# Joining turned token planes on ScalarE, and turning the fourth expert's tokens by DMA, in a mixture of experts behind banded attention

## The chip, the cores and the metric

The kernel runs on one core of one Trainium2 chip. The metric is the device time of one execution in microseconds (us); of several runs the median stands for the kernel. The engines are TensorE (PE in the profile; its weight loads are PEld), VectorE (DVE), ScalarE (ACT), GpSimd (POOL) and SyncE (SP), which issues most of the DMA transfers. GpSimd issues the indirect ones: it gathers rows by a list of indices and scatters them.

## The reference

The input is q, k and v of 8 batches, 8 heads, 576 positions and 64 columns. Attention looks back over a band of 128 positions, with a bias that falls linearly with the distance. Its output, 4608 tokens of 512 columns, goes through eight experts with room for 576 tokens each:

```
scores = where(mask, scale * q @ k.T + bias, -1e9);  x = softmax(scores) @ v
logits = x @ w_gate
for idx in argsort(-logits.flatten()):          # all pairs of token and expert, best first
    tok, e = idx // 8, idx % 8
    if assigned[tok] >= 0 or counts[e] >= 576: continue
    assigned[tok] = e; counts[e] += 1
for e in range(8):
    out[assigned == e] = maximum(x[assigned == e] @ w1[e], 0) @ w2[e]     # 512 -> 1024 -> 512
```

The assignment is greedy over all pairs, so which tokens an expert gets depends on which experts are full already.

## The kernel before, in words

The first part of the span is attention, which writes x to DRAM and the logits to SBUF. Then the router works in eight phases. Each phase finds which expert fills next and the list of its tokens; phase k + 1 runs while expert k is computed. The experts are worked in the order in which they fill. Below they are e0 to e7 in that order, so e3 is the fourth.

**One expert** has two layers, L1 and L2. A matmul of two float32 values is made of three matmuls of their rounded high and low parts. L1 (function `layer1`, matmuls on L1059) works on 8 blocks f of 128 hidden columns, each of two halves of 288 tokens and 12 matmuls a half: 192 matmuls of 288 columns. ScalarE writes the high part of the block (hh, L1064) with the relu, VectorE the low part (hlo, L1069). The halves go through four banks of PSUM. L2 (`layer2`, L1087, L1088, L1090) works on 5 blocks t of 128 tokens (the last has 64), 112 matmuls of 512 columns; ScalarE copies each block from the bank po into o (L1094), VectorE does so for the last, and GpSimd scatters it to the output (L1099). Weights are loaded by SP, eight chunks for an expert, and split into high and low parts by ScalarE (L965) and VectorE (L967, two halves).

**The tokens** of the next expert are gathered by GpSimd, five tiles of 128 (the last of 64), as rows of 512 columns (g, L976). L1 needs them with columns across partitions: they have to be turned. For e1, e2 and e3 TensorE turns them (`turn`, L1000): four 128x128 transposes a tile into the bank pg, from which ScalarE takes the high part xh (L1003) and VectorE the low part xl (L1004). For e4 to e7 (`turn_by_dma`) GpSimd splits each float32 tile into two planes of 16-bit halves (pl, L1017, two copies a tile), SP turns both by one DMA transfer (tp, L1022), GpSimd joins the halves to float32 words again (xf, L1029, two copies a tile), and ScalarE and VectorE take xh (L1037) and xl (L1038). g, pl, tp and xf share one ring of seven buffers.

**The router's steps** are a chain between VectorE and TensorE: VectorE builds compare results and one-hot rows (among them L586, ind; L812, loOH; L808 and L809, mv), TensorE counts with them (L610, L630, L786, L787), and the last step (L817, 18 short matmuls of 128x40) makes the list of tokens out of loOH and mv.

**The order.** Expert k's matmuls are cut into slots, i = 0 to 15 in L1 (12 matmuls) and 16 to 30 in L2 (nine matmuls, six where t is 4). At the end of each slot the function `slot(k, i)` puts other work into the program by tables: `W_LOAD` and `W_SPLIT` say at which slot of which expert a chunk of weights is loaded and split, `WAITS` how many slots lie between two steps of the router, and `DMA_AT` at which slots the generator `turn_by_dma` is taken a step further: its first step issues the gathers, the next five split, the next five turn, and the rest join and take high and low parts. `BY_DMA` is the first expert k in whose time the next one's tokens are turned by DMA. A scheduler then sets the order of every engine's own queue out of this program and its model of times; each engine works its queue strictly in that order. A dependency of the kind `BEHIND` only tells this scheduler to put one instruction behind another. Such a one puts the turning transfers behind the last weight load of L2.

Of the kernel before, what the change touches and what calls it, by code (L numbers as in the profile page):

```python
# [6 lines left out]
F32R = mybir.dt.float32r  # L7
# [3 lines left out]
AF = mybir.ActivationFunctionType  # L11
# [6 lines left out]
CAP = N // E  # L18
# [403 lines left out]
WAITS = (2, 1, 3, 1, 1, 3, 3)  # L422
TURN_WAIT, TURN_STEP = (6, 3), (1, 2)
TURN0 = 3
BY_DMA = 3
DMA_AT = [0, 1, 1, 2, 2, 2, 7, 7, 7, 7, 7, 9, 9, 10, 10, 10, 17, 19, 21, 23, 25]
BEHIND = mybir.DependencyInfo(mybir.DependencyClass.NoSync, mybir.DependencyReason.SCHED_ONLY)
BIG = 1e30
MAGIC = 12582912.0
# [11 lines left out]
def bc(ap, shape):  # L441
    return ap.to_broadcast(shape)
# [17 lines left out]
class Router:  # L460
# [255 lines left out]
    def phase(self, k, exact=False):  # L716
        nc, rt, rs = self.nc, self.p["rt"], self.p["rs"]
# [93 lines left out]
        for a, z in ((0, 18), (18, 30), (30, NT)) if k == 0 else ((0, NT),):  # L811
            nc.vector.tensor_tensor(loOH[:, a:z], bc(self.C["i64"].rearrange("p (s o) -> p s o", o=2).unsqueeze(1), [128, z - a, 32, 2]),  # L812
                                    bc(slo[:, a:z].unsqueeze(2), [128, z - a, 32, 2]), ALU.is_equal)
        yield WAITS[6] + (k < 4)
        ip = self.bank()
        for c in range(0, NT, 2):
            self.last_pe = nc.tensor.matmul(ip[:, 0:40], loOH[:, c:c + 2].rearrange("p c s o -> p (c s o)"),  # L817
# [11 lines left out]
        if k < 7:  # L829
            self.pen = self.small("pen", 8)  # L830
            nc.vector.tensor_scalar(self.pen, Dc, float(CAP), -BIG, ALU.is_ge, ALU.mult)
            self.base = self.small("base", 8)
            nc.vector.tensor_tensor(self.base, self.pen, Dc, ALU.add)
            nc.vector.scalar_tensor_tensor(self.left, keyv, mx[:, 0:1], self.left, ALU.not_equal, ALU.mult)
            L2 = rt.tile([128, 8, NT], F32, name="L2", bufs=1)
            eng = nc.vector if k == 0 or k > BY_DMA else self.tc.nc.gpsimd
            eng.tensor_tensor(L2, L, bc(self.pen.unsqueeze(2), [128, 8, NT]), ALU.add)
            if k == 0 or k > BY_DMA:
                nc.vector.scalar_tensor_tensor(self.L1, T1, 100.0 * BIG, L2, ALU.mult, ALU.add)
            else:  # L840
                Lt = rt.tile([128, 8, NT], F32, name="Lt", bufs=1)
                eng.tensor_scalar(Lt, T1, 100.0 * BIG, 1.0, ALU.mult, ALU.mult)
                eng.tensor_tensor(self.L1, Lt, L2, ALU.add)
# [103 lines left out]
class MoE:  # L947
# [60 lines left out]
    def turn_by_dma(self, idx, asked):  # L1008

        nc, ring = self.nc, self.p["g"]  # L1010
        gs, pls, tps, xfs = self.gather(idx), [], [], []
        yield
        for g, r in gs:
            pl = ring.tile([128, 2, DM], U16, name="pl", tag="g")
            words = g.bitcast(U16).rearrange("q (c o) -> q c o", o=2)
            for a in range(2):
                nc.gpsimd.tensor_copy(pl[:r, a, :], words[:r, :, 1 - a])  # L1017
            pls.append((pl, r))
            yield
        for pl, r in pls:  # L1020
            tp = ring.tile([128, 8, 128], U16, name="tp", tag="g")
            asked.append(nc.sync.dma_start_transpose(tp[:, :, :r], pl[:r].rearrange("q a c -> q (a c)")))  # L1022
            tps.append((tp, r))
            yield
        for tp, r in tps:
            xf = ring.tile([128, 4, 128], F32, name="xf", tag="g")
            words = xf.rearrange("q j t -> q (j t)").bitcast(U16).rearrange("q (j t o) -> q j t o", j=4, o=2)
            for a in range(2):
                nc.gpsimd.tensor_copy(words[:, :, :r, 1 - a], tp[:, 4 * a:4 * a + 4, :r])  # L1029
            xfs.append((xf, r))  # L1030
            yield
        xh = self.p["xg"].tile([128, 4, CAP], F32R, name="xh")
        xl = self.p["xg"].tile([128, 4, CAP], F32R, name="xl")
        self.xg = xh, xl
        for h, (xf, r) in enumerate(xfs):
            o = slice(128 * h, 128 * h + r)
            nc.scalar.copy(xh[:, :, o], xf[:, :, :r])  # L1037
            nc.vector.tensor_tensor(xl[:, :, o], xf[:, :, :r], xh[:, :, o].bitcast(F32), ALU.subtract)  # L1038
            yield

    def layer1(self, w1, xg, first=False):
        nc = self.nc
        xh, xl = xg

        hh = self.p["h"].tile([128, 8, 640], F32R, name="hh")
        hl = self.p["h"].tile([128, 8, 512], F32R, name="hlo")
        cut = (0, 256, 576) if first else (0, 288, 576)
        order = [(f, (0, 1)) for f in range(8)] if not first else [(f, (t,)) for t in range(2) for f in range(8)]
        for f, ts in order:
            w = w1[f // 2].rearrange("p a (j f) -> p a j f", j=4)  # L1050
            fo = (f % 2) * 128
            pp = {t: self.p["ps_h"].tile([128, 512], F32, name="ph")[:, 0:cut[t + 1] - cut[t]] for t in ts}
            todo = [(j, a, x) for j in range(4) for a, x in ((0, xh), (0, xl), (1, xh))]
            if first and f == 0:

                todo.sort(key=lambda p: p[2] is xl)
            for i, (j, a, x) in enumerate(todo):
                for t in ts:
                    nc.tensor.matmul(pp[t], w[:, a, j, fo:fo + 128], x[:, j, cut[t]:cut[t + 1]], start=(i == 0), stop=(i == 11))  # L1059
                if i == 5 and len(ts) == 2:  # L1060
                    yield
            for t in ts:
                o = hh[:, f, cut[t]:cut[t + 1]]
                nc.scalar.activation(o, pp[t], AF.Relu)  # L1064
                e = min(512, cut[t + 1])
                for c0, c1, d in ((cut[t], e, hl[:, f, cut[t]:e]), (e, cut[t + 1], hh[:, f, 576:640])):
                    if c0 < c1:
                        c0, c1 = c0 - cut[t], c1 - cut[t]
                        nc.vector.scalar_tensor_tensor(d, pp[t][:, c0:c1], 0.0, o[:, c0:c1].bitcast(F32), ALU.max, ALU.subtract)  # L1069
            yield  # L1070
        self.h = hh, hl

    def layer2(self, w2, h, idx, last=False):
        nc = self.nc
        hh, hl = h
        for t in range(5) if not last else (4, 0, 1, 2, 3):
            r = 128 if t < 4 else 64

            cols = (slice(0, 256), slice(256, 512)) if last and t == 3 else (slice(0, 512),)
            o = self.p["o"].tile([128, DM], F32, name="o")  # L1080
            for cs in cols:
                po = self.p["ps_o"].tile([128, 512], F32, name="po")
                for f in range(8):
                    w = w2[f // 2].rearrange("p a (c d) -> p a c d", c=2)
                    wh, wl = w[:, 0, f % 2, cs], w[:, 1, f % 2, cs]
                    a, out = hh[:, f, 128 * t:128 * t + 128], po[:, cs]
                    nc.tensor.matmul(out, a, wh, start=(f == 0), stop=False)  # L1087
                    nc.tensor.matmul(out, a, wl, start=False, stop=(f == 7 and t == 4))  # L1088
                    if t < 4:
                        nc.tensor.matmul(out, hl[:, f, 128 * t:128 * t + 128], wh, start=False, stop=(f == 7))  # L1090
                    if f in (2, 5):
                        yield
                if t < 4:
                    nc.scalar.copy(o[:, cs], po[:, cs])  # L1094
                else:
                    o2 = self.p["o"].tile([64, DM], F32, name="o2", bufs=1)
                    nc.vector.tensor_copy(o2, po[64:128, :])
                    nc.vector.tensor_tensor(o[0:64, :], po[0:64, :], o2, ALU.add)
            self.sent = nc.gpsimd.indirect_dma_start(out=self.out, out_offset=bass.IndirectOffsetOnAxis(ap=idx[:r, t:t + 1], axis=0),  # L1099
                                              in_=o[:r, :], in_offset=None)  # L1100
            yield
# [49 lines left out]
def layer_moe(tc, P, C, r, x, w1, w2, out, exact):  # L1151
# [26 lines left out]
    st = dict(wait=START, turn=0)  # L1178
    raws, loaders = {}, {}

    def slot(k, i):
# [18 lines left out]
        for e, layer, c, due in W_SPLIT:  # L1200
            e += k
            if i >= due and len(W.get((e, layer), (0,) * 9)) == c and len(raws[e, layer]) > c:
                W[e, layer].append(m.split(raws[e, layer][c]))
                break
        if k >= BY_DMA and k + 1 in r.idx:
            if k not in gathers:
                asked[k + 1] = []
                gathers[k], st["made"] = m.turn_by_dma(r.idx[k + 1], asked[k + 1]), 0
            while st["made"] < len(DMA_AT) and i >= DMA_AT[st["made"]]:
                next(gathers[k])  # L1210
                st["made"] += 1
        elif i >= 16 and k + 1 in r.idx:
            if k not in gathers:
                gathers[k], st["turn"] = m.turn(m.gather(r.idx[k + 1])), i + TURN_WAIT[min(k, 1)]
            elif i >= st["turn"]:
                next(gathers[k], None)
                st["turn"] = i + TURN_STEP[min(k, 1)]

    gathers, asked = {}, {}
    for k in range(E):  # L1220
        i = 0
# [96 lines left out]
```

## Time and profile before

| | before |
|---|---|
| median of 3 runs | 692.46 us (691.09 to 694.73) |
| the profiled execution | 690.85 us |
| its span, first to last instruction | 688.9 us |
| TensorE busy, mean granted clock | 657.4 us (95%), 0.984 |
| VectorE, ScalarE, GpSimd busy | 479.1 (70%), 332.1 (48%), 192.7 us (28%) |
| L1 and L2 of e2 begin | 356.64 and 385.30 us |
| L1 and L2 of e3 | 415.99 and 443.80 us |
| L1 and L2 of e4 | 471.17 and 498.25 us |
| L1 and L2 of e5 | 526.54 and 553.11 us |
| L1 and L2 of e6, L1 and L2 of e7 | 579.48, 605.06, 630.47 and 656.05 us |

Times in the rows of the profile are us from the start of the span. A row of the timeline gives start, duration, engine, line, operation, what is written and read, shapes and count (neighbours of one kind are put together), and in brackets how long the engine stood before it and what released it. A row of the groups gives line, engine, operation, shapes and count, then busy us and mean ns, then the engine's idle time before such instructions and its releasers. Matmuls are pipelined: one starts before the one ahead of it has ended.

### The profile page before, as it was taken

To read this page: it belongs to the slowest core of one execution; us is meant where nothing else is said; L and a number is where in the kernel's file an instruction comes from. 1 tells how busy PE (TensorE), PEld (TensorE's weight loads), DVE (VectorE), ACT (ScalarE), POOL (GpSimd) and SP (SyncE) were. 2 spreads that over 40 slices of the span, in tenths; PEclk is the share of its full clock that TensorE was granted. 3 is DMA by queue.
4 is the path that set the end of the run, shared out by engine and by line. 5 is a ranking of instruction groups with operands and counts; after the bars stand their busy time and mean duration, and the time that the engine had idled before them with its cause. 6 is when DMAs were issued, how large, how long until landed. Compare 5 with 4: busy or idle time off the path is not lost.

```text
span 688.9 us, 18916 instructions
## 1 busy us (share of the span) xinstructions
PE 657.4 (95%) x7171; PEld 582.2 (85%) x7172; DVE 479.1 (70%) x1985; ACT 332.1 (48%) x991; POOL 192.7 (28%) x376
## 2 busy tenths in 40 slices
PE   7999999999995699999999999999989999999995
PEld 4898998998985399889789779979978978988985
DVE  5788888888887899879669788886775734532310
ACT  6898888888884262334134224324323333432210
POOL 4021221211220301511422017255076075152011
PEclk9999999999997799999999999999999999999998
DMA  8456566566532453615417227635625644621001
GB/s 307 148 181 202 175 193 200 166 211 186 161 106 70 124 191 104 241 39 187 158 36 245 88 92 245 131 106 182 133 98 166 167 111 169 160 52 54 1 25 49
DMA packets 54212, 97.47 MB, mean 141 GB/s; under 512 B 22880, under 2 KB 32224, under 8 KB 54112
## 3 DMA queue, kind: packets, MB, share of 16 engines
q1 hardware_dynamic: 48224, 77.30, 37.0%
q0 software_dynamic: 5888, 18.88, 8.3%
q8 instruction: 58, 0.95, 0.6%
q14 instruction: 42, 0.34, 0.1%
HBM read 72.57 MB, written 18.87 MB: 133 GB/s over the span
## 4 chain that ended last, share of the span: by engine, by line
PE 77%; DVE 12%; DMA 6%; issue 2%; ACT 1%; SPq 1%; POOL 0%; POOLq 0%; DVEq 0%; ACTq 0%
PE ph L1059 20%; PE po L1087 9%; PE po L1088 9%; PE s L54 8%; PE pt L54 7%; PE pt L158 7%; PE po L1090 7%; PE x L54 6%; DMA raw<-in_w_dram 2%; DVE hl L967 2%; DMA tp<-pl 1%; DVE hlo L1069 1%; DMA craw<-in_cst_dram 1%; PE pg L1000 1%; DMA qk<-in_qk_dram 1%
## 5 line engine op out<-in xcount | busy, mean ns | idle before, releaser
L1059 PE MATMUL ph<-xh,hl 128*128 128x288 f32 (+2 forms) x1024 | 188.9, 299 | 0.7 <-DVE lo L534 0.5
L1059 PEld LDWEIGHTS ph<-xh,hl 128*128 128x128 f32 x1024 | 154.7, 189 | 2.4 <-ACT hh L1064 1.0
L145 ACT ACTIVATE u<-u,mn 128x192 f32<-128x192 f32 (+2 forms) x288 | 123.9, 433 | 24.6 <-DVE mn L134 24.5
L1087 PE MATMUL po<-hl,hh 128*128 128x512 f32 (+1 forms) x328 | 128.9, 393 | 0.6 <-ACT o L1094 0.6
L1088 PE MATMUL po<-hl,hh 128*128 128x512 f32 (+1 forms) x328 | 126.4, 385 | 0.0
L967 DVE TENSOR_TENSOR hl<-raw,hl 128x512 fp32r<-128x512 f32 x128 | 88.1, 708 | 48.6 <-ACT hl L965 48.1
L1059 PE MATMUL ph<-xl,hl 128*128 128x288 f32 (+2 forms) x512 | 115.1, 297 | 0.0
L1064 ACT ACTIVATE hh<-ph 128x288 fp32r<-128x288 f32 (+2 forms) x128 | 46.6, 408 | 131.9 <-PE ph L1059 128.8
L134 DVE CUSTOM_DVE_ANT_0 u<-s,bm 128x192 f32<-128x192 f32 x308 | 86.5, 333 | 29.8 <-PE s L54 29.2
L1090 PE MATMUL po<-hl,hlo 128*128 128x512 f32 (+1 forms) x264 | 101.3, 384 | 0.0
L1099 POOL DMA_INDIRECT out_dram<-o,idx x40 | 42.5, 1063 | 153.1 <-ACT o L1094 76.0
L1059 PEld LDWEIGHTS ph<-xl,hl 128*128 128x128 f32 x512 | 84.1, 189 | 0.0
L965 ACT CAST hl<-raw 128x1024 fp32r<-128x1024 f32 x64 | 65.8, 1050 | 25.1 <-DMA raw<-in_w_dram 22.0
L1069 DVE SCALAR_TENSOR_TENSOR hlo<-ph,hh 128x288 fp32r<-128x288 f32 (+2 forms) x128 | 49.4, 417 | 35.8 <-ACT hh L1064 35.1
L1087 PEld LDWEIGHTS po<-hl,hh 128*128 128x128 f32 x328 | 61.8, 188 | 12.3 <-ACT o L1094 1.0
L54 PE MATMUL s<-qk 64*64 64x192 f32 (+1 forms) x1112 | 69.6, 319 | 2.5 <-DVE mn L134 1.8
L1088 PEld LDWEIGHTS po<-hl,hh 128*128 128x128 f32 x328 | 61.8, 188 | 11.0
L1094 ACT COPY o<-po 128x512 f32<-128x512 f32 (+1 forms) x33 | 18.8, 572 | 95.7 <-PE po L1090 77.4
L976 POOL DMA_INDIRECT g<-x,idx x40 | 42.1, 1053 | 72.2 <-issue 31.7
L1090 PEld LDWEIGHTS po<-hl,hlo 128*128 128x128 f32 x264 | 49.6, 188 | 10.0
L158 PE MATMUL pt<-ident_sb,u 128*128 128x128 f32 x368 | 54.2, 282 | 1.4 <-DVE mn L134 1.0
L54 PEld LDWEIGHTS s<-qk 64*64 64x64 f32 x1112 | 48.3, 132 | 8.3 <-issue 2.2
(240 smaller groups left out, 925.8 us busy)
## 6 DMA issues: line engine op xcount, KB each, us to landing
raw<-in_w_dram SPq DMA_DIRECT2D x64, 512.0 KB, 4.4
qk<-in_qk_dram SPq DMA_DIRECT2D x32, 576.0 KB, 4.8
v<-in_v_dram SPq DMA_DIRECT2D x32, 288.0 KB, 3.8
x<-xb SPq DMA_DIRECT2D x14, 512.0 KB, 3.5
x<-xb SPq DMA_DIRECT2D x8, 128.0 KB, 3.3
x<-xb SPq DMA_DIRECT2D x4, 256.0 KB, 2.4
g<-x,idx POOLq DMA_INDIRECT x40, 3.9
out_dram<-o,idx POOLq DMA_INDIRECT x40, 3.2
```

The costliest lines, as they stand in the source:

```text
L54: put(nc.tensor.matmul(out, w, a, start=start, stop=stop, skip_group_check=True))
L134: put(nc.vector.tensor_tensor_reduce(out=u[rows], in0=x[rows, c:c + 64 * m].rearrange("q (j k) -> q j k", k=64), in1=bm[n % NP][rows, y:y ...
L145: put(nc.scalar.activation(u, u, AF.Exp, bias=st["mn"][:, i:i + 1], scale=-1.0, accum_out=st["sm"][:, i:i + 1]))
L158: put(nc.tensor.transpose(ps[:, c:c + 128], u[:, o + 128 * j:o + 128 * j + 128], ident))
L965: self.last = nc.scalar.copy(hl[:, 0, :], raw)
L967: nc.vector.tensor_tensor(hl[:, 1, c:c + 512], raw[:, c:c + 512], hl[:, 0, c:c + 512].bitcast(F32), ALU.subtract)
L1059: nc.tensor.matmul(pp[t], w[:, a, j, fo:fo + 128], x[:, j, cut[t]:cut[t + 1]], start=(i == 0), stop=(i == 11))
L1064: nc.scalar.activation(o, pp[t], AF.Relu)
L1069: nc.vector.scalar_tensor_tensor(d, pp[t][:, c0:c1], 0.0, o[:, c0:c1].bitcast(F32), ALU.max, ALU.subtract)
L1087: nc.tensor.matmul(out, a, wh, start=(f == 0), stop=False)
L1088: nc.tensor.matmul(out, a, wl, start=False, stop=(f == 7 and t == 4))
L1090: nc.tensor.matmul(out, hl[:, f, 128 * t:128 * t + 128], wh, start=False, stop=(f == 7))
```

## The change

The tokens of e3 are turned by DMA as those of e4 to e7 are (`BY_DMA` from 3 to 2); their gathers, splits and turning transfers are put into the program from slot 10 to 13 of e2's L1, and their joins from slot 23 to 27, in L2. The two joining copies of a tile go from GpSimd to ScalarE, and join, xh and xl of a tile are now one step; each join stands, for the scheduler, behind the latest relu or output copy on ScalarE (`acted`). The steps of the joins of e4 to e7 move from slots 9, 10 and 17 to 25 to slots 18 to 26. The wait ahead of the router's last step (L817) is one slot longer from phase 4 on. Which phases leave their list bookkeeping (L835 to L843) to GpSimd stays as it was: `k > BY_DMA` and `k > 3` are the same under the two values.

```diff
-BY_DMA = 3
-DMA_AT = [0, 1, 1, 2, 2, 2, 7, 7, 7, 7, 7, 9, 9, 10, 10, 10, 17, 19, 21, 23, 25]
+BY_DMA = 2
+DMA_AT = {2: [10, 11, 11, 12, 12, 12, 13, 13, 13, 13, 13, 23, 24, 25, 26, 27], 3: [0, 1, 1, 2, 2, 2, 7, 7, 7, 7, 7, 18, 20, 22, 24, 26]}
...
-        yield WAITS[6] + (k < 4)
+        yield WAITS[6] + 1
...
-            eng = nc.vector if k == 0 or k > BY_DMA else self.tc.nc.gpsimd
+            eng = nc.vector if k == 0 or k > 3 else self.tc.nc.gpsimd
...
-        for tp, r in tps:
+        xh = self.p["xg"].tile([128, 4, CAP], F32R, name="xh")
+        xl = self.p["xg"].tile([128, 4, CAP], F32R, name="xl")
+        self.xg = xh, xl
+        for h, (tp, r) in enumerate(tps):
             xf = ring.tile([128, 4, 128], F32, name="xf", tag="g")
             words = xf.rearrange("q j t -> q (j t)").bitcast(U16).rearrange("q (j t o) -> q j t o", j=4, o=2)
             for a in range(2):
-                nc.gpsimd.tensor_copy(words[:, :, :r, 1 - a], tp[:, 4 * a:4 * a + 4, :r])
-            xfs.append((xf, r))
-            yield
-        xh = self.p["xg"].tile([128, 4, CAP], F32R, name="xh")
-        xl = self.p["xg"].tile([128, 4, CAP], F32R, name="xl")
-        self.xg = xh, xl
-        for h, (xf, r) in enumerate(xfs):
+                joined = nc.scalar.copy(words[:, :, :r, 1 - a], tp[:, 4 * a:4 * a + 4, :r])
+                self.tc.add_manual_dep(joined.ins, self.acted.ins.name, BEHIND, reason="layers first")
             o = slice(128 * h, 128 * h + r)
             nc.scalar.copy(xh[:, :, o], xf[:, :, :r])
...
-                nc.scalar.activation(o, pp[t], AF.Relu)
+                self.acted = nc.scalar.activation(o, pp[t], AF.Relu)
...
-                    nc.scalar.copy(o[:, cs], po[:, cs])
+                    self.acted = nc.scalar.copy(o[:, cs], po[:, cs])
...
-            while st["made"] < len(DMA_AT) and i >= DMA_AT[st["made"]]:
+            due = DMA_AT[min(k, 3)]
+            while st["made"] < len(due) and i >= due[st["made"]]:
```

Three places of the order show what moves. First TensorE in L2 of e2, near its first third, before (L630 is a step of the router, L1000 four transposes of a token tile):

```order
L1087 MATMUL po<-hl,hh 128x512
L1088 MATMUL po<-hl,hh 128x512
L1090 MATMUL po<-hl,hlo 128x512
L630 LDWEIGHTS c_ones
L630 MATMUL m<-sat_81,c_ones 128x1
L1000 MATMUL pg<-ident_sb,g 128x128 x4
L1087 MATMUL po<-hl,hh 128x512
```

In the change the five groups L1000 of this layer are gone, and nothing stands in their place; the steps L817 stand nine matmuls later in L2 of e3 and e4.

Second GpSimd from the end of e2's L1 to L2 of e4: out_dram is the scatter of an output block, g the gather of a token tile, pl the split, xf the join. Before, from the scatters of e2's L2 on:

```order
L1099 DMA out_dram<-o,idx 4608x512 x3
L976 DMA g<-x,idx 128x512
L1099 DMA out_dram<-o,idx 4608x512
L976 DMA g<-x,idx 128x512 x3
L976 DMA g<-x,idx 64x512
L1017 COPY pl<-g 128x512 x4
L1099 DMA out_dram<-o,idx 4608x512
L1017 COPY pl<-g 128x512 x4
L1017 COPY pl<-g 64x512 x2
L1029 COPY xf<-tp 128x512 x8
L1029 COPY xf<-tp 128x4x64 x2
L1099 DMA out_dram<-o,idx 4608x512
```

And now, from the gathers of e3's tokens in L1 of e2 on,

```order
L976 DMA g<-x,idx 128x512 x4
L976 DMA g<-x,idx 64x512
L1017 COPY pl<-g 128x512 x8
L1017 COPY pl<-g 64x512 x2
L1097 DMA out_dram<-o,idx 4608x512 x4
```

and further on, from three scatters in e3's L2:

```order
L1097 DMA out_dram<-o,idx 4608x512 x3
L976 DMA g<-x,idx 128x512 x4
L976 DMA g<-x,idx 64x512
L1017 COPY pl<-g 128x512 x2
L1097 DMA out_dram<-o,idx 4608x512
L1017 COPY pl<-g 128x512 x6
L1017 COPY pl<-g 64x512 x2
```

Ten splits stand directly behind the gathers in L1 of e2, the ten joins are gone, and the gathers for e5 stand behind three scatters of e3's L2, with eight of their splits behind a fourth.

Third ScalarE in L2 of e3. Before (L1064 is the relu of L1, L1037 takes xh, L965 rounds weights, L1094 copies an output block):

```order
L1064 ACTIVATE hh<-ph 128x288 x4
L1037 CAST xh<-xf 128x4x128 x4
L1037 CAST xh<-xf 128x4x64
L965 CAST hl<-raw 128x1024
L1094 COPY o<-po 128x512 x4
L965 CAST hl<-raw 128x1024 x4
```

And now:

```order
L1092 COPY o<-po 128x512
L1032 COPY xf<-tp 128x512 x3
L1035 CAST xh<-xf 128x4x128
L1032 COPY xf<-tp 128x512
L1035 CAST xh<-xf 128x4x128
L1092 COPY o<-po 128x512
L1032 COPY xf<-tp 128x512 x2
L1035 CAST xh<-xf 128x4x128
L1092 COPY o<-po 128x512
L1032 COPY xf<-tp 128x512 x2
L1032 COPY xf<-tp 128x4x64
L1035 CAST xh<-xf 128x4x128
```

The first xh stood ahead of the output copies; now joins and casts stand between them, the first behind the first output copy.

More of the change, by code (lines that the diff above doesn't have):

```diff
@@ L835, in phase @@
             L2 = rt.tile([128, 8, NT], F32, name="L2", bufs=1)
-            eng = nc.vector if k == 0 or k > BY_DMA else self.tc.nc.gpsimd
+            eng = nc.vector if k == 0 or k > 3 else self.tc.nc.gpsimd
             eng.tensor_tensor(L2, L, bc(self.pen.unsqueeze(2), [128, 8, NT]), ALU.add)
-            if k == 0 or k > BY_DMA:
+            if k == 0 or k > 3:
                 nc.vector.scalar_tensor_tensor(self.L1, T1, 100.0 * BIG, L2, ALU.mult, ALU.add)
```

## The prediction, made before the change was run

> **What bounds the kernel now.** I write e0 to e7 for the eight experts in their order, and L1 and L2 for the two layers of one expert. I read the page first, then the busy time by stage, one window for each layer of each expert, then what TensorE waited for between 356.64 and 582 us.
>
> ```profile
> PE 657.4 (95%) x7171; PEld 582.2 (85%) x7172; DVE 479.1 (70%) x1985; ACT 332.1 (48%) x991; POOL 192.7 (28%) x376
> ```
>
> TensorE is busy 95% of the span, so only its own work, or time in which it stands, can be won. The stages show where there is some. Columns: window, its length, busy time of PE, PEld, DVE, ACT and POOL with counts, the granted clock, the DMA share and GB/s.
>
> ```profile
> 356.64:385.30 28.66, 27.25 (x223) 26.50 (x221) 27.01 (x108) 9.80 (x19) 7.48 (x8) 1.00 0.58 194
> 385.30:415.99 30.69, 30.11 (x173) 23.27 (x172) 23.42 (x102) 9.04 (x15) 5.57 (x5) 1.00 0.20 67
> 443.80:471.17 27.37, 26.28 (x134) 21.44 (x133) 20.81 (x69) 9.20 (x15) 19.42 (x26) 1.00 0.31 102
> 498.25:526.54 28.29, 26.34 (x134) 21.45 (x133) 15.13 (x34) 9.31 (x15) 22.51 (x28) 1.00 0.33 104
> 605.06:630.47 25.41, 25.41 (x114) 21.03 (x113) 7.43 (x13) 8.80 (x14) 12.05 (x14) 1.00 0.15 48
> 630.47:656.05 25.58, 25.58 (x193) 25.58 (x192) 8.65 (x25) 5.00 (x14) 0.90 (x1) 1.00 0.03 6
> ```
>
> The last two windows are layers without routing or turning beside them: 25.4 us for L2 and 25.6 for L1. Against these, L2 of e2 is 5.3 us too long, L2 of e3 2.0, L2 of e4 2.9, and L1 of e2 3.1. Nothing that the change does can win more than such excess. VectorE is busy 27.01 of 28.66 us in L1 of e2: there it has no room. The waits name the releasers (total, times, longest):
>
> ```profile
> PE m L817 <- DVE mv L809: 3.0, 2, 1.9
> PE m L610 <- DVE ind L586: 0.7, 1, 0.7
> PE po L1087 <- ACT o L1094: 0.6, 1, 0.6
> PE m L787 <- DVE run L780: 0.3, 1, 0.3
> ```
>
> **The turns leave TensorE: a gain of 3.0 us.** In L2 of e2, five groups of four transposes (L1000) go. First the row of L1000 alone in that window, then the one group that also waits:
>
> ```profile
> 385.30:415.99 30.69, 2.98 (x20) 2.08 (x20) 1.00 0.20 67
> 407.23 0.66 PE L1000 MATMUL pg<-ident_sb,g 128*128 128x128 f32 x4 [0.58 <-DVE xl L1004]
> ```
>
> Busy 2.98 plus the wait of 0.58 is 3.6 at most; each group's first and last transpose run under its neighbours' ends, some 0.1 to 0.2 us a group, so 2.6 at least. I take 3.0.
>
> **The last router step goes one step later from e3 on: a gain of 3.0 us.** The step L817 needs the one-hot rows loOH and mv from VectorE. Where it waits, and VectorE before the second wait:
>
> ```profile
> 452.72 0.61 PE L817 MATMUL m<-mv,loOH 128*128 128x40 bf16 x18 [1.09 <-DVE mv L809]
> 508.06 0.61 PE L817 MATMUL m<-mv,loOH 128*128 128x40 bf16 x18 [1.95 <-DVE mv L809]
> 500.85 0.69 DVE L1038 TENSOR_TENSOR xl<-xf,xh 128x512 fp32r<-128x512 f32 x1 [0.86 <-ACT xh L1037]
> 505.75 1.57 DVE L812 TENSOR_TENSOR loOH<-c_i,slo 128x2304 bf16<-128x2304 bf16 x1
> ```
>
> One slot is nine matmuls of L2, 9 x 25.41 / 112 = 2.0 us, so it covers 1.09 and 1.95 by itself. Besides, in the second place VectorE stood 0.86 us and more behind an xl whose xf GpSimd had not joined; the order now puts the xl's behind loOH. I take the whole 3.0; if loOH came later too, by what the next part costs, 1 to 2 of it would be kept, which is the lower end.
>
> **The joins move to ScalarE: nothing, and 0.6 us gained.** What GpSimd paid, and what ScalarE pays for a copy of that size:
>
> ```profile
> L1029 POOL COPY xf<-tp 128x512 uint16<-128x512 uint16 x32 | 27.2, 914 | 61.1 <-DMA tp<-pl 60.7
> L1017 POOL COPY pl<-g 128x512 uint16<-128x512 uint16 x32 | 18.8, 628 | 0.2 <-DMA g<-x,idx 0.2
> L1094 ACT COPY o<-po 128x512 f32<-128x512 f32 x31 | 18.0, 585 | 91.0 <-PE po L1090 72.6 <-issue 16.0 <-PE m L630 1.7
> L1037 ACT CAST xh<-xf 128x512 fp32r<-128x512 f32 x16 | 9.9, 621 | 18.7 <-POOL xf L1029 18.7
> DMA to landing us min/median/max: 2.6/3.8/6.0
> ```
>
> ScalarE has not made a 16-bit join in this trace. Its nearest rows are the 512-wide copies of 0.585 and 0.621; the upper end is GpSimd's 0.914. Ten joins (eight full, two half) cost 5.3 us, at most 8.5, in an L2 of 25.4 where ScalarE is busy 8.8 to 9.3. So it ends near 15, at most 18, of 25.4. What hides it: each join stands behind the copy of an output block (one every 5.1 us), so three or four joins and a cast, 2.4 to 3.0 us, fit before the next is due. The transfers land 3.8, at most 6.0 us after their issue, and the last of a group is issued by the start of L2; the first join starts some 5.7 us into L2. What waits behind a join that waits is the next output copy and, through it, a bank of po; the 0.6 us on L1094 in the list above came from casts that stood ahead of it in L2 of e5, and those now stand behind it. If the cover were gone, each join of an L2 would count, up to 5.3 us an expert.
>
> **GpSimd's splits move beside VectorE's busy time: a loss of 4.9 us.** This is what speaks against the change. The splits (pl, L1017) of e3's tokens are new in L1 of e2, right behind the last gather; and, by the order, the gathers of e3 to e5's L2 now stand behind three output scatters, so that eight of the ten splits fall into the first 7 us of the next L1. In the trace one run of splits lies on VectorE's chain already, in L1 of e3 (two rows of GpSimd, six of VectorE, and then two operations at rest):
>
> ```profile
> 424.94 1.16 POOL L1017 COPY pl<-g 128x512 uint16<-128x512 uint16 x2
> 426.27 2.55 POOL L1017 COPY pl<-g 128x512 uint16<-128x512 uint16 x4 [0.17 <-DMA g<-x,idx]
> 424.13 0.69 DVE L967 TENSOR_TENSOR hl<-raw,hl 128x512 fp32r<-128x512 f32 x1
> 424.80 1.85 DVE L967 TENSOR_TENSOR hl<-raw,hl 128x512 fp32r<-128x512 f32 x1
> 426.58 0.58 DVE L883 TENSOR_SCALAR fy<-fq,bq 128x16 f32<-128x16 f32 x1
> 427.19 0.52 DVE L884 TENSOR_SCALAR fy<-fy 128x16 f32<-128x16 f32 x1
> 427.75 0.56 DVE L886 TENSOR_SCALAR kf<-fy 128x32 bf16<-128x32 f32 x1
> 428.34 1.03 DVE L586 TENSOR_TENSOR ind<-kf,c_i 128x1024 bf16<-128x1024 bf16 x1
> 384.94 0.23 DVE L883 TENSOR_SCALAR fy<-fq,bq 128x16 f32<-128x16 f32 x1
> 382.51 0.68 DVE L586 TENSOR_TENSOR ind<-kf,c_i 128x1024 bf16<-128x1024 bf16 x1
> ```
>
> L967 takes 1.85 beside the splits against 0.69 just before (+1.16), L586 1.03 against 0.68 (+0.35), L883 0.58 against 0.23 (+0.35), and L884 and L886 about as much: 2.6 us lost in 3.7 us of splits, a share of 0.7. The mild end is the start of L1 in e4, where the splits end in the middle of three L967:
>
> ```profile
> 465.41 5.51 POOL L1017 COPY pl<-g 128x512 uint16<-128x512 uint16 x9
> 469.74 2.33 DVE L967 TENSOR_TENSOR hl<-raw,hl 128x512 fp32r<-128x512 f32 x3 [5.81 <-ACT hl L965]
> ```
>
> They overlap 1.2 us (469.74 to 470.92), and the three take 2.33 against 3 x 0.69: 0.26 lost, a share of 0.2. Between 0.2 and 0.7 I take 0.4, since the chain mixes operations of both kinds.
>
> In L1 of e2 the last gather is issued by 378.4 us, and L586, for which TensorE waits 0.7 us already, ended at 383.2:
>
> ```profile
> 377.51 0.91 POOL L976 DMA_INDIRECT g<-x,idx  x1 [0.30 <-issue]
> ```
>
> Ten splits are 6.3 us; with the chain stretched some 5.5 of them lie ahead of L586. All of it counts, as the wait is there already: 5.5 x 0.4 = 2.2 us (1.1 to 3.9). At the heads of L1 in e4, e5 and e6 what is late next is the low part of the first hidden block (hlo, L1069), whose bank the third block of matmuls needs when the second is done:
>
> ```profile
> 475.98 0.74 DVE L1069 SCALAR_TENSOR_TENSOR hlo<-ph,hh 128x288 fp32r<-128x288 f32 x2
> 477.62 0.71 ACT L1064 ACTIVATE hh<-ph 128x288 fp32r<-128x288 f32 x2 [2.49 <-PE ph L1059]
> ```
>
> It and the 64-wide piece behind it end at 476.85, and the second block's end shows at 477.6: 0.75 us of slack. About 3.5 us of splits lie ahead of it: 3.5 x 0.4 - 0.75 = 0.65 us in e4 and e6 each (0 to 1.7). In e5 the step L787 has no slack (the 0.3 us in the list of waits): 1.4 (0.7 to 2.5). Together 2.2 + 1.3 + 1.4 = 4.9 us (1.8 to 9.7).
>
> [...]
>
> **The sum.** Gains 3.0 + 3.0 + 0.6 = 6.6 us, losses 4.9: 1.7 us less. The profiled execution took 690.85 us, its span 688.9 and 1.95 around it; 690.85 - 1.7 = 689.15. The median of the runs, 692.46, lies 1.6 above the profiled execution: 690.8. A share of 0.2 gives 6.6 - 1.8 = 4.8 less, 687.7; one of 0.7 gives 9.7 - 6.6 = 3.1 more, 695.5.
>
> **Rivals.** First, **the splits cost nothing**: the scheduler's order isn't the chip's time, and if the splits fall where VectorE waits for other things the whole 6.6 us stay: 685.9. For it: VectorE is busy only 15.13 of 28.29 us in L2 of e4; against it: the 27.01 of 28.66 in L1 of e2. Chance 0.23.
>
> Second, on the other side, **the wait in L1 of e2 lets the clock fall**. Before the experts the trace shows such a fall:
>
> ```profile
> 213.59 1.47 PE L54 MATMUL pt<-wn_sb,xT 128*128 128x144 f32 x10
> 216.00:217.00 1.00, 0.00 (x0) 0.93 0.75 225
> 233.00:234.00 1.00, 1.00 (x4) 0.54 0.33 131
> ```
>
> TensorE stops at 215.06, the grant falls within the next 2 us (mean 0.93 from 216 to 217), and is back only in 233 to 234. At a share of 0.7 the wait for L586 grows from 1.1 to 5 us in one piece; that is the point from which it decides, as the 1.95 us before L817 passed at full clock. [...] Chance 0.12. [...]
>
> Third, **ScalarE's joins are slow** (1.5 us and more, as the slowest of GpSimd's): output copies and casts of the weights then come late in four L2's, 1.5 us or more in each: 697. Against it stand the 0.585 rows. Chance 0.04.
>
> Fourth, **the waits at L817 stay**, because the splits delay loOH by the same slot: 690.8 + 3.0 = 693.8. Chance 0.08.
>
> **Chances and range.** My case has 0.53, with a range of its own from 687.7 to 695.5. A measurement of this kernel can tell about 0.5%, 3.5 us, from no change: faster is below 689.0, slower above 695.9. Of my case 0.15 lies below 689.0. Faster: 0.23 + 0.15 = 0.38. Slower: 0.12 + 0.04 = 0.16. The same: the other 0.38 of mine and 0.08, 0.46. The range, 685.2 to 696.5, takes in the first and fourth rival and leaves out the second and third, 0.16, and some 0.03 of tails.
>
> **What would show it.** In the profile after: no L1000 in L2 of e2 and that layer near 27.5 us; no wait on L817 in L2 of e3 and e4; joins of 0.55 to 0.65 us on ScalarE, and no wait of po on L1094 above 0.6; splits from about 378.4 in L1 of e2, with L967 and the small operations at two to three times their quiet length, and the wait before L610 at about 3 us; splits in the first 7 us of L1 in e4 to e6 and TensorE standing there about 0.5 to 1.5 us. The prediction is wrong if L1 of e2 keeps its 28.7 us (the first rival), if the granted clock falls below 1 after 380 us (the second), or if TensorE waits for xl or o in any L2.

## The result

| | before | the change |
|---|---|---|
| median | 692.34 us (691.09 to 694.73, 4 runs) | 712.56 us (708.37 to 715.97, 4 runs) |
| ratio | | 1.0285 (1.0212 to 1.0358) |
| span of the profiled execution | 688.9 us | 714.2 us |
| mean granted clock | 0.984 | 0.958 |

The change is 2.9% slower. The forecast was 690.8 us with a range from 685.2 to 696.5. Times here and below are of fast runs; one run of the kernel before, 802.8 us at a mean clock of 0.747, and one of experiment 5, 714.0 us, were slow and are left out.

The page of the changed kernel first: TensorE has 20 transposes less and is still busy 13.6 us longer, with 94% of a longer span.

```profile
PE 671.0 (94%) x7151; PEld 593.6 (83%) x7152; DVE 493.8 (69%) x1985; ACT 361.1 (51%) x1041; POOL 163.8 (23%) x346
```

More busy time with less work goes with the lower granted clock, 0.958 against 0.984: the share of its full speed at which TensorE was let run. The busy time by stage, with the columns of the prediction's table (the sixth entry is the granted clock): L1 and L2 of e2, e3, e4, e5, then L1 of e6.

```profile
360.24:395.62 35.38, 30.34 (x223) 28.95 (x222) 33.06 (x110) 9.68 (x19) 13.11 (x18) 0.90 0.65 189
395.62:423.01 27.39, 27.39 (x154) 21.53 (x152) 21.25 (x96) 14.16 (x24) 5.45 (x5) 1.00 0.24 80
423.01:456.11 33.10, 30.49 (x222) 29.14 (x220) 26.84 (x81) 9.87 (x20) 12.24 (x16) 0.90 0.66 168
456.11:482.27 26.16, 26.16 (x134) 21.36 (x133) 17.62 (x67) 15.04 (x25) 8.45 (x10) 1.00 0.37 114
482.27:515.22 32.95, 29.91 (x221) 28.97 (x220) 26.03 (x78) 9.29 (x19) 7.35 (x11) 0.90 0.59 145
515.22:541.42 26.20, 26.20 (x134) 21.37 (x133) 12.80 (x34) 15.04 (x25) 8.42 (x10) 1.00 0.38 114
541.42:573.34 31.92, 28.18 (x215) 27.72 (x214) 24.24 (x60) 9.28 (x19) 7.15 (x11) 0.95 0.59 155
573.34:598.75 25.41, 25.41 (x115) 21.02 (x113) 6.81 (x12) 15.06 (x25) 8.42 (x10) 1.00 0.38 112
598.75:629.77 31.02, 27.57 (x194) 27.16 (x192) 19.81 (x36) 9.27 (x19) 7.35 (x11) 0.94 0.61 149
```

Every L2 has won: 3.3, 1.2, 2.1 and 1.0 us, 7.6 in all, against lengths of 30.69, 27.37, 28.29 and 26.37 before. Every L1 has lost: 6.7, 5.3, 5.9, 5.4 and 5.4 us, 28.7 in all (before: 28.66, 27.81, 27.08, 26.57, 25.58). The balance is +21.1 us of the 25.3 between the two spans. Another 3.6 us lie ahead of e2, where the two programs are the same: e2 began at 360.24 instead of 356.64, and in the executions below anywhere between 355.9 and 360.1. This profiled execution has a stretch at a clock of 0.50 from 13 to 23 us, in attention, which that of the kernel before doesn't have; so these 3.6 us are not the change's.

What TensorE waited for from e2 on:

```profile
PE ph L1057 <- DVE hlo L1067: 12.0, 4, 4.3
PE m L786 <- DVE ei L773: 3.4, 1, 3.4
PE m L630 <- DVE sat L627: 1.1, 1, 1.1
```

These 16.5 us are one long wait for VectorE in each L1 (two in e3's). In all TensorE stood 17.9 us in these five layers, by the windows above, and 1.6 before; so 16.3 of the 28.7 us are waits. The other 12.4 are a longer busy time, and nearly all of it is work at half clock: TensorE's busy time from e2 on in windows of 1 us, times what is missing there to a clock of 1, gives 12.2. VectorE at the places of these waits, in L1 of e2 and of e4, and GpSimd's splits beside them:

```profile
381.58 5.94 DVE L861 TENSOR_SCALAR q<-q,half,rw 128x36 f32<-128x36 f32 x1
381.86 5.62 POOL L1017 COPY pl<-g 128x512 uint16<-128x512 uint16 x10
484.49 4.70 DVE L967 TENSOR_TENSOR hl<-raw,hl 128x512 fp32r<-128x512 f32 x1
484.14 4.50 POOL L1017 COPY pl<-g 128x512 uint16<-128x512 uint16 x8
```

L861 works on 36 columns and takes 0.30 us at rest (at 378.16 in the kernel before). Here it starts before the ten splits and ends 0.04 us after them; L967, at rest 0.69 us, starts in the first of eight splits and ends 0.55 us after the last. VectorE didn't take turns with the copies of these two rows: it stood until the row was through, 5.94 and 4.70 us. (In L1 of e3 of experiment 2 it did take turns.)

TensorE in L1 of e2, and the granted clock there (window, length, PE busy, clock, DMA share, GB/s):

```profile
388.62 0.61 PE L1057 MATMUL ph<-xh,hl 128*128 128x288 f32 x1 [4.31 <-DVE hlo L1067]
388.00:389.00 1.00, 0.38 (x1) 0.75 1.06 197
394.00:395.00 1.00, 1.00 (x6) 0.50 0.40 75
395.00:396.00 1.00, 1.00 (x7) 0.84 0.77 130
```

The clock falls to one half near 388.5, just ahead of the first matmul at 388.62, and returns near 395.3: 6.8 us at half clock behind a wait of 4.3.

### The profile page after: what moved, and what is told of

The parts are those of the page before. It is cut to its first block, busy times and chain, and to the rows that moved or that the text cites. A ratio compares the mean times of both kernels' runs of the same rounds, so it can differ in the third digit from the quotient of the medians.

```text
span 714.2 us, 18921 instructions
## 1 busy us (share of the span) xinstructions
PE 671.0 (94%) x7151; PEld 593.6 (83%) x7152; DVE 493.8 (69%) x1985; ACT 361.1 (51%) x1041; POOL 163.8 (23%) x346
## 4 chain that ended last, share of the span: by engine, by line
PE 72%; DVE 17%; issue 5%; ACT 2%; DMA 2%; SPq 0%; POOL 0%; POOLq 0%; DVEq 0%
PE ph L1057 20%; PE s L54 9%; PE po L1085 7%; PE po L1086 7%; PE pt L158 7%; PE pt L54 7%; DVE hl L967 6%; PE po L1088 6%; PE x L54 6%; DMA raw<-in_w_dram 2%; DVE hlo L1067 1%; DVE q L861 1%; ACT xf L1032 1%; DVE u L134 1%; ACT hl L965 1%
## 5 line engine op out<-in xcount | busy, mean ns | idle before, releaser
L1057 PE MATMUL ph<-xh,hl 128*128 128x288 f32 (+2 forms) x1024 | 198.1, 308 | 12.9 <-DVE hlo L1067 12.0
L1057 PEld LDWEIGHTS ph<-xh,hl 128*128 128x128 f32 x1024 | 162.2, 197 | 16.2 <-DVE hlo L1067 12.8
L1057 PE MATMUL ph<-xl,hl 128*128 128x288 f32 (+2 forms) x512 | 119.3, 306 | 0.0
L967 DVE TENSOR_TENSOR hl<-raw,hl 128x512 fp32r<-128x512 f32 x128 | 104.7, 837 | 18.0 <-ACT hl L965 10.6
L134 DVE CUSTOM_DVE_ANT_0 u<-s,bm 128x192 f32<-128x192 f32 x308 | 86.6, 333 | 33.3 <-PE s L54 32.7
L1057 PEld LDWEIGHTS ph<-xl,hl 128*128 128x128 f32 x512 | 88.3, 198 | 0.3 <-issue 0.3
L965 ACT CAST hl<-raw 128x1024 fp32r<-128x1024 f32 x64 | 66.1, 1050 | 24.3 <-DMA raw<-in_w_dram 21.0
L54 PE MATMUL s<-qk 64*64 64x192 f32 (+1 forms) x1112 | 71.9, 327 | 1.8 <-DVE mn L134 1.6
L54 PEld LDWEIGHTS s<-qk 64*64 64x64 f32 x1112 | 49.8, 137 | 8.3 <-issue 2.9
```

The source lines that it names most:

```text
L54: put(nc.tensor.matmul(out, w, a, start=start, stop=stop, skip_group_check=True))
L134: put(nc.vector.tensor_tensor_reduce(out=u[rows], in0=x[rows, c:c + 64 * m].rearrange("q (j k) -> q j k", k=64), in1=bm[n % NP][rows, y:y ...
L965: self.last = nc.scalar.copy(hl[:, 0, :], raw)
L967: nc.vector.tensor_tensor(hl[:, 1, c:c + 512], raw[:, c:c + 512], hl[:, 0, c:c + 512].bitcast(F32), ALU.subtract)
```

## The experiments

The first four were run together, the next four together, the last two together; the kernel before ran beside each (medians 693.2, 693.7 and 693.8 us). Theory A is that the splits on GpSimd hold VectorE for their whole row and the clock falls on top; the other theories are named where they are tried.

**1. The splits on ScalarE, spread.** The prime suspect is taken off GpSimd, the rest of the change stays.

```diff
-DMA_AT = {2: [10, 11, 11, 12, 12, 12, 13, 13, 13, 13, 13, 23, ...], 3: [0, 1, 1, 2, 2, 2, 7, 7, 7, 7, 7, 18, ...]}
+DMA_AT = {2: [10, 12, 13, 14, 15, 17, 17, 17, 17, 17, 17, 23, ...], 3: [0, 2, 4, 6, 8, 10, 10, 10, 10, 10, 10, 18, ...]}
...
-                nc.gpsimd.tensor_copy(pl[:r, a, :], words[:r, :, 1 - a])
+                cut = nc.scalar.copy(pl[:r, a, :], words[:r, :, 1 - a])
+                self.tc.add_manual_dep(cut.ins, self.acted.ins.name, BEHIND, reason="layers first")
```

> The changed kernel, but the splits (pl) are made by ScalarE instead of GpSimd, each behind the latest relu or output copy, and spread: one tile in every second slot of L1 for e4 on, and from slot 12 to 17 of e2's L1 for e3. [...] Theory B (the fuller queue of ScalarE makes weight casts and relus late, and VectorE with them): ten more copies on ScalarE make it worse: 712 us or more.

Theory A had about 686 us (683 to 690) for this kernel, with the clock at 1.0 and no VectorE operation longer than about 1 us. Measured: 685.43 us (683.47 to 687.36), ratio to before 0.9885 (0.9834 to 0.9937). The L1 of e2, e3, e4, e5 and e6:

```profile
358.37:388.09 29.72, 27.73 (x222) 26.56 (x221) 27.65 (x110) 12.91 (x25) 7.47 (x8) 1.00 0.56 187
415.50:444.18 28.68, 27.61 (x222) 26.68 (x220) 22.78 (x81) 15.13 (x30) 6.19 (x6) 1.00 0.66 180
470.34:497.47 27.13, 27.13 (x222) 26.56 (x221) 20.84 (x77) 14.43 (x29) 1.73 (x2) 1.00 0.62 168
523.66:550.20 26.54, 26.46 (x214) 26.15 (x213) 19.03 (x59) 14.43 (x29) 1.68 (x2) 1.00 0.67 183
575.62:601.39 25.77, 25.77 (x194) 25.61 (x193) 14.55 (x35) 14.43 (x29) 1.68 (x2) 1.00 0.67 176
```

The five fall from 35.4, 33.1, 33.0, 31.9 and 31.0 to 29.7, 28.7, 27.1, 26.5 and 25.8, the clock is 1.00 in all of them, and ScalarE, with more work than in the change, holds TensorE up once, for 0.5 us in L1 of e2. Theory B falls. This kernel is faster than both. The edit moves the splits to another engine and also spreads them; the two weren't tried apart, but experiments 8 and 10 work on GpSimd's splits alone.

**2. The joins back on GpSimd.**

```diff
-                joined = nc.scalar.copy(words[:, :, :r, 1 - a], tp[:, 4 * a:4 * a + 4, :r])
-                self.tc.add_manual_dep(joined.ins, self.acted.ins.name, BEHIND, reason="layers first")
+                nc.gpsimd.tensor_copy(words[:, :, :r, 1 - a], tp[:, 4 * a:4 * a + 4, :r])
```

> The changed kernel, but the joins are made by GpSimd again. Theory A: the splits stand where they stand in the changed kernel, in L1 of e2 all ten in a row and in L1 of the later ones at least five, so the stalls stay: L1 of e2 about 35 us, 703 to 716 us in all. Theory B: ScalarE's queue is as before, so the stalls in the L1 of e3 to e6 go, about 690 us.

Measured: 703.75 us (703.04 to 705.37), 1.0165 (1.0112 to 1.0217), at the low end of what theory A expected. With ScalarE's queue as it was, three of the five stalls stay: L1 of e2, e4 and e5 take 33.1, 29.9 and 31.1 us. There is a new one, 4.7 us before L610 in L2 of e2, where the joins lie beside the router's chain.

Two L1's lose nothing. In e6 (25.6 us) all ten splits are done before the layer begins at 592.95. In e3 (27.2 us, clock 1.00) seven of them lie inside it without a gap, and there VectorE does take turns, against theory A:

```profile
435.38 5.26 POOL L1017 COPY pl<-g 128x512 uint16<-128x512 uint16 x7
435.90 1.02 DVE L967 TENSOR_TENSOR hl<-raw,hl 128x512 fp32r<-128x512 f32 x1
437.46 0.52 DVE L884 TENSOR_SCALAR fy<-fy 128x16 f32<-128x16 f32 x1
438.02 0.53 DVE L886 TENSOR_SCALAR kf<-fy 128x32 bf16<-128x32 f32 x1
```

Each of these operations is slower than at rest (0.68 us for L967, 0.17 and 0.18 for L884 and L886, medians of the kernel before), but it stands for one copy and not for the row. So a row of copies without a gap stopped VectorE for its whole length in the change, 5.94 us for ten copies, and didn't here.

**3. e3's tokens turned by TensorE.**

```diff
-BY_DMA = 2
+BY_DMA = 3
```

> The changed kernel, but e3's tokens are turned by TensorE as before (BY_DMA = 3). Both theories: L1 of e2 loses its stall of 4.5 us and its half clock (35.4 us back to about 28.7), L2 of e2 takes the turns back (27.4 to about 30.7): 3.4 us less, 709 us. Theory A has the excess of 5.7 to 7.8 us in the L1 of e3 to e6 unchanged, since their splits are; it falls if those are much smaller.

Measured: 708.21 us (703.20 to 712.82), 1.0200 (1.0136 to 1.0263). The three layers L1 and L2 of e2 and L1 of e3:

```profile
360.06:389.61 29.55, 27.48 (x223) 26.55 (x221) 27.20 (x108) 9.91 (x19) 7.47 (x8) 1.00 0.56 188
389.61:420.20 30.59, 30.01 (x173) 23.40 (x172) 23.62 (x102) 9.16 (x15) 6.42 (x6) 1.00 0.22 74
420.20:452.11 31.91, 28.97 (x222) 28.11 (x220) 25.39 (x77) 9.14 (x19) 10.17 (x15) 0.95 0.65 173
```

L1 of e2 is 5.8 us shorter than in the change and L2 3.2 longer, so the turn of the fourth expert's tokens by DMA costs 2.6 us on balance in these two layers, and L1 of e3 1.2 more. The stalls of e4 to e6 are another part's: these L1's take 33.2, 32.0 and 31.4 us here.

**4. The router's step one slot later, alone,** on the kernel before.

```diff
-        yield WAITS[6] + (k < 4)
+        yield WAITS[6] + 1
```

> The kernel before, with the wait ahead of the router's last step one slot longer from phase 4 on, and nothing else of the change. Both theories: the waits at L817 in L2 of e3 and e4 (1.09 and 1.95 us) go, the rest stays: 3.0 us less, about 689.4 us (688 to 691).

Measured: 699.10 us (695.49 to 704.82, 9 runs), 1.0092 (1.0056 to 1.0128). A miss by 10 us, with the sign wrong. One wait at L817 goes and 0.8 us of the other stays, but the list of tokens comes later (the gathers in L2 of e3 begin 16.0 us into the layer instead of 13.9), and the last five splits fall behind a scatter into the head of e4's L1:

```profile
477.78 2.82 POOL L1017 COPY pl<-g 128x512 uint16<-128x512 uint16 x5
477.52 3.62 DVE L967 TENSOR_TENSOR hl<-raw,hl 128x512 fp32r<-128x512 f32 x1
484.09 1.10 PE L1059 MATMUL ph<-xh,hl 128*128 128x288 f32 x2 [2.07 <-DVE hlo L1069]
```

In the kernel before they ran from 465.4 on, into the quiet end of L2. L1 of e4 has grown from 27.1 to 31.0 us, that of e5 from 26.6 to 30.1.

**5. A pause between any two splits,** a memset of one column.

```diff
-                nc.gpsimd.tensor_copy(pl[:r, a, :], words[:r, :, 1 - a])
+                cut = nc.gpsimd.tensor_copy(pl[:r, a, :], words[:r, :, 1 - a])
+                if pause is not None:
+                    self.tc.add_manual_dep(cut.ins, pause.ins.name, BEHIND, reason="pause")
+                pause = nc.gpsimd.memset(rest, 0.0)
+                self.tc.add_manual_dep(pause.ins, cut.ins.name, BEHIND, reason="pause")
```

> The changed kernel, with a write of one column (memset, no read of SBUF) on GpSimd between any two splits. [...]

Two theories stood against each other. A1: a break in the row lets VectorE in, however short it is; the longest operation in L1 of e2 falls from 5.94 to below 1.5 us, 695 to 701 us in all. A2: such a break changes nothing, 709 to 716 us. Measured: 700.33 us (696.57 to 706.54, 8 runs), 1.0104 (1.0063 to 1.0145). The time is at the upper end of A1's, but VectorE didn't do what A1 says: L861 still takes 3.88 us in L1 of e2, from 377.88 to 381.76, and this L1 33.5 us. GpSimd there:

```profile
381.08 0.60 POOL L1018 COPY pl<-g 128x512 uint16<-128x512 uint16 x1
381.63 0.09 POOL L1021 MEMSET rest<- 128x1 f32 x1
381.93 0.61 POOL L1018 COPY pl<-g 128x512 uint16<-128x512 uint16 x1 [0.22 <-DMA g<-x,idx]
```

Behind the first five memsets the next split begins 0.03 to 0.04 us after the memset has begun, and L861 goes on standing. Behind the sixth GpSimd waits 0.22 us for a gather, and there L861 gets through. So in this row writes of 0.09 to 0.10 us didn't let VectorE in, and a gap of 0.22 us did. At the heads of the later L1's the two engines took turns in places: the wait in L1 of e6 is gone and that of e5 is 0.7 us, that of e4 still 3.3.

**6. The change with the router's step where it was.**

```diff
-        yield WAITS[6] + 1
+        yield WAITS[6] + (k < 4)
```

> The changed kernel, with the wait ahead of the router's last step as before. Theory C (the step moved by a slot makes the list, the gathers and with them the splits late, so that they fall beside VectorE's work at the head of L1): the splits of e4 to e6 lie some 2 us earlier, the stalls in L1 of e4, e5 and e6 fall from 3.5 to 4.1 us to about 2, the waits at L817 come back in part: about 707 us. If the scheduler's place of the gathers behind the scatters sets it alone: the stalls stay, 712 us or more.

Measured: 709.04 us (708.09 to 711.37), 1.0219 (1.0159 to 1.0278). The time lies between what the two theories expected, but the waits decide: in L1 of e4, e5 and e6 they are what they were (3.0, 3.4 and 3.3 us with the change and here). Theory C falls for the change: there something else sets the place of the gathers. And L817 doesn't wait in L2 of e3 and e4.

**7. The same step back where the splits are on ScalarE** (the edit of experiment 6 on the kernel of experiment 1).

> The kernel with the splits spread on ScalarE, with the wait ahead of the router's last step as before. All theories: without splits on GpSimd the step's own worth is seen, the waits of 1.09 and 1.95 us at L817 come back: 3.0 us more than that kernel's 685.4, 688.4 us. Less, if the joins on GpSimd were half of what made loOH late.

Measured: 688.60 us (686.97 to 691.29, 9 runs), 0.9928 (0.9902 to 0.9953). The time is the expected one and the reason isn't. L817 in L2 of e3 and of e4 has no wait in front:

```profile
452.49 0.62 PE L817 MATMUL m<-mv,loOH 128*128 128x40 bf16 x18
506.00 0.62 PE L817 MATMUL m<-mv,loOH 128*128 128x40 bf16 x18
```

So the waits of 1.09 and 1.95 us don't need the moved step to go: they went with the new place of the joins, on ScalarE and at later slots. These two weren't tried apart; in experiment 2, with the joins on GpSimd at the later slots and the step moved, the waits are gone as well. The 3 us lie in L1 of e3, 31.3 us instead of 28.7, with a wait of 1.7 us before L630 (1.1 in experiment 1) and 3.4 us at half clock behind it. Why that wait is longer with the step back wasn't tried.

**8. Every split twice.**

```diff
                 nc.gpsimd.tensor_copy(pl[:r, a, :], words[:r, :, 1 - a])
+                nc.gpsimd.tensor_copy(pl[:r, a, :], words[:r, :, 1 - a])
```

> The changed kernel, with every split made twice. Theory A (VectorE stands for the whole row): the longest VectorE operation in L1 of e2 grows from 5.94 to about 11.5 us, at the head of e4 from 4.70 to about 9; TensorE stands 4 to 6 us more in each of five L1's: 735 to 745 us. If GpSimd and VectorE took turns, VectorE's single operations would stay as long as they are and only more of them would be slow.

Measured: 737.98 us (two runs, 737.97 and 738.00), 1.0632 (1.0560 to 1.0705). In L1 of e2:

```profile
378.40 11.48 DVE L861 TENSOR_SCALAR q<-q,half,rw 128x36 f32<-128x36 f32 x1
```

Twice the row, twice the stand: 11.48 against 5.94 us. In this row taking turns is excluded.

**9. The joins of e4 to e7 sooner.** g, pl, tp and xf share a ring of seven buffers.

```diff
-7, 7, 7, 7, 7, 18, 20, 22, 24, 26]}
+7, 7, 7, 7, 7, 16, 17, 18, 19, 20]}
```

> The changed kernel, with the joins of e4 to e7 put at slots 16 to 20 instead of 18 to 26. Theory D (g, pl, tp and xf share a ring of seven buffers; joins that end late keep the next gathers waiting for buffers, so the scheduler puts them behind the third output block, and their splits fall into the head of L1): the gathers of e5 to e7 begin one output block, about 5 us, sooner, most splits lie in the tail of L2 where VectorE has little to do, the stalls of 3.5 to 4.1 us in L1 of e4, e5 and e6 shrink to about 1 and the clock stays up there; e2 and e3 keep theirs: 697 to 702 us. If the later list alone sets the place of the gathers: 709 to 714 us.

Measured: 696.94 us (693.99 to 697.95), 1.0052 (1.0020 to 1.0085). The gathers in L2 of e3 begin at 464.32 there, 13.4 us into the layer; in the change at 475.54, 19.4 us into it:

```profile
464.32 0.97 POOL L976 DMA_INDIRECT g<-x,idx  x1 [5.05 <-issue]
475.54 0.98 POOL L976 DMA_INDIRECT g<-x,idx  x1 [0.30 <-issue]
```

The L1 of e4, e5 and e6 are 28.5, 27.4 and 25.6 us instead of 33.0, 31.9 and 31.0. What theory D expected came in all three places, the gathers, the stalls and the time: with late joins the scheduler puts the next gathers behind the third output block, and with sooner ones behind the first. That the shared ring of buffers is the link is argued from the program; its size wasn't varied.

**10. Only e3's splits on GpSimd,** the rest as in experiment 1.

```diff
+                if k == 2:
+                    nc.gpsimd.tensor_copy(pl[:r, a, :], words[:r, :, 1 - a])
+                    continue
                 cut = nc.scalar.copy(pl[:r, a, :], words[:r, :, 1 - a])
```

> The kernel with the splits spread on ScalarE, but the ten splits of e3's tokens, in L1 of e2, on GpSimd and at the slots of the change. Theory A: this is the change's stall in L1 of e2 alone. L1 of e2 goes from 29.7 to about 35 us, one VectorE operation there takes 5 to 6 us, the clock falls once, the L1 of e4 to e6 stay at 27.1, 26.5 and 25.8: 685.4 + 5.6 = 691 us.

Measured: 690.26 us (686.95 to 693.60, 10 runs), 0.9950 (0.9925 to 0.9975). L1 of e2 is 33.3 us long, with one stand of VectorE:

```profile
381.28 3.70 DVE L861 TENSOR_SCALAR q<-q,half,rw 128x36 f32<-128x36 f32 x1
```

The row was broken here by a gather that came late, so the stand was 3.7 and not 5 to 6 us. The stall in e2 alone costs 4.8 us against experiment 1.

## Why the prediction was wrong, point by point

**The turns (3.0 us): right.** L2 of e2 is 3.3 us shorter.

**The router's step (3.0 us): right in size, wrong in cause.** The waits at L817 are gone. Experiments 6 and 7 show them gone with the step where it was, experiment 4 shows 0.8 us left with the step moved alone. With the joins' new place no xl stands ahead of loOH on VectorE any more, which the prediction named as the second reason; how much the engine and how much the later slots do in this is open. The step moved alone costs 6 us, which the prediction didn't ask.

**The joins on ScalarE (nothing, 0.6 gained): right, with a price too low.** Fifty joins:

```profile
L1032 ACT COPY xf<-tp 128x512 uint16<-128x512 uint16 (+1 forms) x50 | 32.2, 712 | 0.0
```

A full one takes 0.77 us in the median (a half one 0.48), between the 0.585 taken and the 0.914 of the upper end; ScalarE is busy 15.0 of 25.4 us in L2, as estimated, and nobody waits there. L2 of e5 lost its 1.0 us of excess.

**The splits beside VectorE (a loss of 4.9 us, at most 9.7): here the prediction failed.** The loss is 28.7 us. Three steps went wrong.

First, the share of 0.4. It was taken from two stretches that were not like the new rows. In the first, L967 with its 1.85 us stood until the pair of splits from 424.94 on was done and got in at a gap of 0.17 us, in which GpSimd waited for a gather; the small operations behind it then took turns with single splits. In the second only the last two splits of the row met VectorE, and the two engines took turns, GpSimd waiting first: those two splits take 1.62 us instead of the 1.2 of a quiet pair. In the rows that the change made, one VectorE operation stood for the whole row, a share of 1, and experiment 8 shows it by doubling. That GpSimd had waited in the second stretch, so that the 0.26 us were no measure of VectorE's loss, was to be seen in its own timeline of the kernel before:

```profile
469.30 1.62 POOL L1017 COPY pl<-g 128x512 uint16<-128x512 uint16 x2
```

With a share of 1, as these rows show it, the prediction's own sum of splits (5.5 us in e2, 3.5 less 0.75 of slack in e4 and e6, 3.5 in e5) comes to 14.5 us, without a term for e3; the waits in L1 of e2, e4, e5 and e6 are 14.1 us (4.31, 3.04, 3.43 and 3.32).

Second, L1 of e3 wasn't in the sum at all. Its splits had run beside VectorE before as well, and TensorE waited 0.2 us in all there. Now two L967 stand there for 2.55 and 2.38 us, each behind three splits in a row, TensorE waits 1.4 and 1.1 us, the clock falls, and the layer is 5.3 us longer.

Third, the clock. It was a rival of 0.12, and its decision point, a wait near 5 us, was the author's estimate. It fell in all five L1's, for 6.8 us each in e2, e3 and e4 and 3.4 us each in e5 and e6, and cost 12.2 us. The rival had the right cause and side. The windows of full clock behind the 1.95 us at L817 were taken as proof that such a wait is safe; in experiment 4 a wait of 2.07 us and in experiment 7 one of 1.74 us brought the clock down. What sets these apart is in the last section.

Why the splits came to those places is told by experiments 3, 6 and 9: in e2 because they were put there, in e4 to e6 because the joins now end late (and, by theory D, hold the ring). The prediction saw both in the order and priced them wrongly.

## What to carry to other kernels

Here ten copies on GpSimd that followed one another without a gap stopped VectorE for their whole length, 5.94 us for an operation on 36 columns that takes 0.30 at rest; so price such a row at its full length, not at a share of it, and put it where VectorE has nothing that TensorE waits for, or on another engine. The same ten splits on ScalarE, one tile between two relus, turned a loss of 2.9% into a gain of about 1%. Before a stage is made later, look for what shares its buffers: here later joins moved the next gathers, and these moved the splits. And price a wait of TensorE from about 1.7 us on with the risk of 3.4 us at half clock behind it: 1.74 us brought that in experiment 7.

## What the runs showed of the hardware

**A row of copies on GpSimd stopped VectorE in some places and not in others.** In L1 of e2, e4, e5 and e6 of the change one VectorE operation stood to the end of the row (5.94, 4.70, 4.71 and 4.71 us); a gap in which GpSimd waited for a gather let it in (0.17 us in the kernel before, 0.22 in experiment 5, 0.67 in experiment 10), a one-column memset of 0.09 to 0.10 us inside the row of experiment 5 didn't. In L1 of e3 of experiment 2 (0.52 and 0.53 us for L884 and L886), and in the kernel before at 427.19 and 427.75 (0.52 and 0.56 us for the same), an operation got in behind a single copy although the next one followed at once. What decides is open. Starting first didn't: L861 in the change starts 0.28 us ahead of the first split.

**In these profiles the half clock came in pieces of 3.4 us, and a fall went with the standing inside one such piece.** In the changed kernel the stretches from e2 to e6 at half clock add up to 6.8, 6.8, 6.8, 3.4 and 3.4 us, in experiment 4 to twice 3.4, in experiment 8 to 10.2, 10.2, 10.2, 6.8 and 10.2 us. A fall showed before the work was back, as at 388.5 above, or after: at 610.4 in the change the work had been back since 608.62. Waits of much the same length did and didn't bring it: 1.95 us in the kernel before didn't, 1.74 us in experiment 7 did.

The traces tell these apart. Within each profile the falls and returns lie whole multiples of 3.41 us apart, so they mark off pieces of that length. Take all pieces from 250 us to the last layer, in the twelve profiles, that begin at full clock. With 1.74 us or more of standing TensorE, by the modelled ends of its matmuls, a piece ended in a fall in 26 of 26 cases; with less than 1.48 us none did; of the six between, three did. The fall that the prediction shows before the experts fits: TensorE stood 1.8 us in the piece that ends at 216.85. The 1.95 us before L817 lay across two pieces, with 0.86 and 1.08 us of standing (length, then PE busy; the granted clock is the third number from the end):

```profile
503.57:506.98 3.41, 2.55 (x12) 1.77 (x10) 3.41 (x6) 1.24 (x2) 3.41 (x5) 1.00 0.00 0
506.98:510.40 3.42, 2.34 (x26) 2.13 (x27) 3.42 (x9) 1.84 (x3) 1.27 (x2) 1.00 0.00 0
```

The 1.74 us of experiment 7 lay in one, and the next piece is at half clock:

```profile
422.00:425.42 3.42, 1.68 (x14) 1.44 (x13) 1.76 (x11) 2.38 (x5) 0.00 (x0) 1.00 1.00 310
425.42:428.83 3.41, 3.41 (x16) 3.41 (x15) 3.04 (x8) 2.04 (x5) 0.00 (x0) 0.50 0.41 144
```
